# Two opening loads moved to ScalarE's queue, with another hand-written list of steps

## The chip, the cores and the metric

The kernel runs on one core of one Trainium2 chip. The metric is the time of one execution on the device, in microseconds. An execution is one launch that computes both blocks of the reference below from inputs in device memory to an output in device memory.

The core has five engines with queues of their own, each working through its instructions in order: TensorE (PE in the profile) for matmuls, VectorE (DVE), ScalarE (ACT), GpSimd (POOL) and SyncE (SP), which here only issues DMAs. ScalarE can issue DMAs too. Semaphores order the engines among each other.

## The reference

A transformer block on 2048 tokens of width 640: a layer norm, an attention with a compressive memory over four segments of 512 tokens, an output projection with a residual, a second layer norm and a feed-forward block of width 1728 with a residual. All tensors are bfloat16.

```python
def _A_ref(x, wq, wk, wv, wo, beta):          # x is the normalised input
    H, Dh, N, L = 32, 20, 4, 512
    q, k, v = ...                              # (x @ w), split in heads and segments
    phi = lambda t: jnp.where(t > 0, t + 1.0, jnp.exp(t))
    ...
    for s in range(N):
        p = softmax(qs @ ks.T * Dh**-0.5 + causal_mask)
        a_dot = p @ vs
        a_mem = (phi(qs) @ M) / (phi(qs) @ z + 1e-6)
        o = g * a_mem + (1.0 - g) * a_dot      # g = sigmoid(beta), per head
        M = M + phi(ks).T @ vs
        z = z + sum(phi(ks))
    return o @ wo

h  = x + _A_ref(layernorm(x), wq, wk, wv, wo, beta)
h2 = h + silu(layernorm(h) @ w1) @ w2
```

## The kernel before

Tokens lie in 16 blocks of 128, four blocks to a segment. A program written in Python declares some 1,400 steps, each with its engine or engines, what it reads and writes, and the buffers that it takes. It then goes through the table `ORDER`, a long string that names every step once, in order, with the engine where there is a choice (`/A` ScalarE, `/D` VectorE, `/G` GpSimd, `/S` SyncE) and the numbers of the buffers that it takes. `schedule` (from line 302) only reads that table; no planner runs. Steps are emitted in the table's order, so each engine's queue is the part of the table that belongs to it, and a class called `Tracker` adds the waits that reads and writes need.

The names in the table that matter here: `x0`, `x1`, `x2`, `x4`, `x8`, `x12` load blocks of tokens from that block on (one, one, two, four, four, four blocks). `w_q0`, `w_q1`, `w_q2` load the query weights in three parts of 128, 256 and 256 rows, `w_k0` and `w_k1` the key weights in two; `w_w1_0` to `w_w1_4` and `w_w2_0` to `w_w2_5` load the feed-forward weights. `n1_stB`, `n1_rB`, `n1_apB` are the statistics, the reciprocal root and the normalising of block B for the first layer norm, `n2_` the same for the second. For blocks 0 to 3 the transposing is done by TensorE (`n1_tp`, copied out by `n1_te`), for all others by a DMA (`n1_tr`, `n2_tr`). `ot` transposes the attention's output and `kt` phi of the keys, also by DMA. `re_wq` and `re_wk` copy the loaded weights into the order of heads that the projections `pr` need. `vt` and `vp` are DMAs that copy the remaining rows of queries and keys, and of phi of the queries, to the partitions where TensorE wants them. `qk` are the scores, `e` their exponentials (a `+` makes one instruction of 2048 columns in place of two of 1024), `mk` the causal masks, `av` the product with the values, `wo`, `h1`, `h2` the later matmuls. `fill` are matmuls on zeros.

In the opening, SyncE issues every load. Block 0's statistics are taken by VectorE (line 742), those of block 1 by ScalarE (lines 734 and 737), whose first instruction is a table load. VectorE then prepares the root for block 1 (line 753), GpSimd takes it (line 763), VectorE normalises (line 769), TensorE transposes (line 778), and after the copy and the first rearranged query weights (line 694) the projections begin (lines 871 and 866). While this goes on, TensorE runs 30 fillers.

The loads' engine is the last argument of `load_x` (line 575) and `load_w` (line 580), which hand it to `dma`. Each engine's DMAs have one hardware queue: SyncE's is q1, ScalarE's q10. The w2 buffer holds the queries and keys of the first segment until they are used (`QZ`, `QZV`), so the loads of w2 wait for the scores of that segment, and what stands behind them on SyncE waits too.

Of the kernel before, what the change touches and what calls it, by code (L numbers as in the profile page):

```python
# [11 lines left out]
PE, AC, DV, PO, SP = "pe", "act", "dve", "pool", "sp"  # L12
# [312 lines left out]
D = 640  # L325
# [43 lines left out]
mk4x1_384 ve02/D lsc2 lsc3 oe0x/D:0 mk4x2_0 mk4x2_256 av2x:7 ex041:1 oe2x/D:1 kt02:0 n1_tr6 mk0y1_256 mm2 kt00:1 v11:0
qk4x30:2 e4x30:3 pha011:0 ve11/D:1 tn0x:6 nm0x:3 e4x32 mk4x3_0 pha031:1 qk0ya0:0 mk4x3_256 n1_ap7:2 mk4x3_384 v12:6  # L370
e0ya+:4 w_w1_2 ve12/D av4x:4 oe4x/D:0 mz00:5 ma00/A:2,5 qk1ya0:0 e1ya2:0 tn2x:6 nm2x:0 av6x:7 oe6x/D:1 e1ya0 tn4x:6
nm4x:1 qk2ya0:2 kvz e2ya2:1 tn6x:7 mm3 nm6x:2 n1_tr4 v10:0 n1_st11:2 e2ya0 qk0y20:4 e0y2+:6 w_w1_3 w_w1_1 mk0y2_0
kg00/G:0 mk0y2_256 n1_tr7 v13:2 n1_r11/G qk3ya0:4 e3ya0:3 ve10/D n1_st9:6 n1_r9/D pha041:2 ex031:2 mm6 ve13/D ot1:0
wo1:0 n1_st8:3 e3ya2 ot0 ex011:0 wo0:2 rs1 n2_st1:0 mk0y1_384 w_w1_4 phb011 qk4ya0:4 e4ya0:2 n2_r1/D kg02/G e4ya2 rs0
n2_ap1:0 n2_st0:0 pr101:0 qe101/A:0 av0y:1 qk0y30:2 e0y3+:0 w_w2_0/S pr120:6 zf0 n2_r0/D oe0y/D:0 pr100:7 mk0y3_0
ex101:0 qk5ya0:2 n2_ap0:3 e5ya2:4 n2_tr1:0 phb041 qe100/D e5ya0 qe120/D:0 pr121:0 qe121/D qk4y10:4 mk0y3_256 tn0y:1
nm0y:3 e4y10:5 e4y12 mk0y3_384 n1_r8/D av2y:0 oe2y/D:1 qk6ya0:2 mk4y1_0 pha120:0 pr141:1 qe141/D:0 phb031 n2_tr0
h1_0_7_0:6 e6ya+:0 th0_7_0:0 s0_7_0:0 h1_0_12_0:0 th0_12_0:1 qk7ya0:1 e7ya+:1 kt01:0 w_w2_5 h1_0_4_0:7 tn2y:5 s0_12_0
h1_0_3_0:6 kg01/G mk4y1_256 n1_st10:1 th0_3_0:0 mk4y1_384 qvz h1_0_6_0:0 qk4y20:1 th0_4_0:1 nm2y:3 s0_4_0 mm4
h1_0_5_0:5 e4y2+:3 s0_3_0 pr110:7 qe110/D:0 th0_5_0:1 qk4y30:1 pr140:6 th0_6_0:0 e4y32:6 mk4y2_0 e4y30 w_w2_1/S  # L380
mk4y2_256 s0_6_0 s0_5_0 mk4y3_0 mk4y3_256 qe140/D av4y:0 kt03:1 kg03/D ex120:1 qk8a0:4 e8a0:2 e8a2 pr111:1 h1_0_1_0:2
th0_1_0:1 oe4y/D:0 h1_0_8_0:3 th0_8_0:0 qe111/D vt10/S:0 qk8e0:4 s0_1_0 n1_ap8:3 e8e0:4 s0_8_0 mz01:0 ma01/D:3,1
mk4y3_384 av6y:1 e8e2 zf1 qk8b0:2 e8b+:5 kh03/D oe6y/D:1 h1_0_10_0:0 th0_10_0:0 tn4y:6 mzc6 n1_ap9:0 mk8e_0 nm4y:2
tn6y:7 kt04:1 mk8a_0 phb120 nm6y:0 ex100:2 pr130:1 qe130/D:0 qk9a0:3 e9a+:0 s0_10_0 kg04/D pr131:2 qe131/D mk8b_0
pha131:0 h1_0_2_0:7 w_w2_2/S kh04/D th0_2_0:1 mm5 h1_0_11_0:1 th0_11_0:0 s0_11_0 qk9b0:2 e9b0:1 s0_2_0 h1_0_0_0:0
mz02:6 pha101:1 vt13/S mk8b_384 th0_0_0:0 e9b2 mk9a_0 mk9b_0 mk8e_256 h1_0_9_0:7 th0_9_0:1 s0_0_0 ma02/D:0,4,6,7
qk10a0:0 e10a0:3 mzc2 h1_0_13_0:6 h2_0_0:4 e10a2 w_w2_4 ot3 h2_0_1 mk9b_384 mk10a_0 phb101 n1_r10/D pha111:2 vt19/S
mzc0 mb00:0,0 w_w2_3/S s0_9_0 n1_ap11:2 pha100:0 phb100 th0_13_0:0 s0_13_0 ex131:0 phb131 pha110:0 n1_ap10:1 vt12/S
qk10b0:0 e10b+:6 epsg1 av8:7 oe8/D:0 n1_tr8:0 av9:6 oe9/D:1 n1_tr9 ex110:0 phb110 vt18/S vt110/S h2_0_2 mk10b_0
mk10b_384 qk10e0:0 e10e2:2 e10e0 n1_tr11 h2_0_3 ex121:0 h2_1_0:6 o0 kt13:0 qk11a0:2 pha121:0 phb121 wo3:0 rs3 n2_st3:3  # L390
mk10e_0 mk10e_256 h2_1_1 e11a+:4 mk11a_0 vt14/S qk11b0:2 kg13/G:0 ex130:1 tn8:0 e11b+:5 h2_1_2 vt11/S h2_1_3 pha140:0
nm8:1,1 o1 kh13/G n2_r3/G ex111:2 phb111 mm1 n2_ap3:2 mk11b_0 mk11b_384 pha130:0 vt16/S mzc1 vt111/S ot2 qk12a0:2
# [70 lines left out]
def build(nc, es, A_x, A_wq, A_wk, A_wv, A_wo, A_beta, B_x, B_w1, B_w2, out):  # L463
# [10 lines left out]
    G = Graph(pools)  # L474
# [48 lines left out]
    mt = sb("mt", [128, V4], F32)  # L523
    zpad = sb("zpad", [128, 256], BF16)
# [48 lines left out]
    sT0 = G.alloc("sT")  # L573
# [851 lines left out]
```

## Time and profile before

| | |
|---|---|
| three runs, us | 297.7, 298.06, 300.65 (median 298.06) |
| profiled execution's own time, us | 298.33 |
| its span, first to last instruction, us | 296.6 |
| granted TensorE clock, mean | 1.000 |
| DMA queue q1 (SyncE) | 48204 packets, 23.18 MB |
| DMA queue q10 (ScalarE) | 1668 packets, 1.74 MB |
| read from and written to device memory | 10.41 MB and 2.62 MB |

The profile is one execution, taken by the hardware profiler. Times in its rows count from the span's start. A row of the timeline merges instructions of one kind that follow each other; a row that ends in "q" and a line number, such as SPq L578, is the issue of DMAs by that engine, not their transfer. Matmuls are pipelined and their ends are modelled, so TensorE's busy time is a little generous. What ended a wait is inferred from semaphore events; for a wait on several, the last is named.

### The profile page before, as it was taken

Reading aid. Unit: us, or ns where it says so; the run is one execution under the profiler, and the core shown is the slowest. Engines: PE = TensorE matmul, PEld = TensorE weight load, DVE = VectorE, ACT = ScalarE, POOL = GpSimd, SP = SyncE. Lnnn points to the kernel's source line nnn. Section 1 sums busy time; section 2 is a strip of 40 time slices with the busy share of each in tenths; the row PEclk is TensorE's granted clock in tenths of the full one; section 3 lists DMA queues with packets and bytes.
Section 4 is the critical chain, followed back from the end, with each engine's and each line's share of the span. In section 5 each row is a group of like instructions: output and inputs, shape, how many; then the busy total and the mean of one; then the engine's idle time right before and its main releaser. Section 6 shows DMA issues by size and latency. Waiting matters only on the chain.

```text
span 296.6 us, 7437 instructions
## 1 busy us (share of the span) xinstructions
PE 285.0 (96%) x2991; PEld 167.6 (56%) x2991; DVE 222.8 (75%) x506; ACT 217.5 (73%) x266; POOL 139.9 (47%) x257
## 2 busy tenths in 40 slices
PE   7897879999999999999999999999999999999997
PEld 5775445545665455566643444465665457764575
DVE  3897889768989789899678967759967688626522
ACT  5875979999999899999879999788759751014400
POOL 6246834744656477646525656355576620200000
PEclk9999999999999999999999999999999999999999
DMA  7968772804943321254462400154181023220002
GB/s 208 366 209 114 192 105 68 221 18 98 168 89 75 74 39 26 37 111 66 97 140 51 77 1 2 26 75 88 20 102 32 0 59 76 68 67 25 22 22 91
DMA packets 49906, 25.40 MB, mean 86 GB/s; under 512 B 39488, under 2 KB 48032, under 8 KB 49872
## 3 DMA queue, kind: packets, MB, share of 16 engines
q1 hardware_dynamic: 48204, 23.18, 37.3%
q10 hardware_dynamic: 1668, 1.74, 1.9%
q8 instruction: 24, 0.39, 0.6%
q14 instruction: 10, 0.08, 0.1%
HBM read 10.41 MB, written 2.62 MB: 44 GB/s over the span
## 4 chain that ended last, share of the span: by engine, by line
PE 76%; DVE 8%; DMA 7%; ACT 4%; POOL 2%; issue 2%; SPq 1%; DVEq 0%; ACTq 0%
PE ps_all L1349 19%; PE ps_all L1307 15%; PE ps_all L866 12%; PE ps_all L1272 7%; PE ps_all L964 7%; PE ps_all L827 5%; PE ps_all L1008 5%; ACT PT L976 3%; DMA x_tok<-in_A_x_dram 3%; DMA xT<-xn_rot 2%; PE ps_all L1038 1%; DMA w_sb<-w_sb 1%; PE ps_all L1092 1%; PE ps_all L1225 1%; POOL PT L987 1%
## 5 line engine op out<-in xcount | busy, mean ns | idle before, releaser
L976 ACT ACTIVATE PT<-ps_all 128x1024 bf16<-128x1024 f32 (+1 forms) x120 | 153.1, 1310 | 17.7 <-PE ps_all L964 16.5
L987 POOL TENSOR_SCALAR_AFFINE_SELECT PT<-PT 128x512 bf16<-128x512 bf16 x128 | 81.5, 647 | 59.1 <-ACT PT L976 57.0
L1349 PE MATMUL ps_all<-w_sb,sT 128*128 128x320 bf16 (+2 forms) x462 | 64.9, 295 | 0.0
L1307 PE MATMUL ps_all<-hT,w_sb 128*128 128x512 bf16 (+1 forms) x325 | 63.0, 337 | 0.5 <-DVE sT L1322 0.4
L1316 ACT ACTIVATE th<-ps_all 128x512 f32<-128x512 f32 (+2 forms) x70 | 34.0, 505 | 35.1 <-PE ps_all L1307 31.0
L1349 PEld LDWEIGHTS ps_all<-w_sb,sT 128*128 128x128 bf16 x462 | 43.2, 98 | 18.3 <-issue 1.8
L1322 DVE SCALAR_TENSOR_TENSOR sT<-th,ps_all 128x512 bf16<-128x512 f32 (+2 forms) x70 | 37.8, 561 | 17.1 <-ACT th L1316 16.1
L1307 PEld LDWEIGHTS ps_all<-hT,w_sb 128*128 128x128 bf16 x325 | 29.8, 98 | 25.9 <-issue 3.2
L763 POOL TENSOR_TENSOR rst<-rst,eps_c 128x1 f32<-128x1 f32 x32 | 18.4, 579 | 25.1 <-DVE rst L757 23.5
L742 DVE BATCH_NORM_STATS2 stt<-x_tok 128x6 f32<-128x320 bf16 x62 | 27.2, 481 | 1.8 <-DMA x_tok<-in_A_x_dram 1.4
L1362 DVE SCALAR_TENSOR_TENSOR x_tok<-ps_all,x_tok 128x640 bf16<-128x640 f32 (+3 forms) x18 | 13.3, 745 | 16.7 <-PE ps_all L1349 16.6
L1070 POOL TENSOR_TENSOR otok<-on 128x320 bf16<-128x320 bf16 x24 | 19.0, 796 | 11.5 <-DVE on L1062 11.5
L1272 PE MATMUL ps_all<-wo_sb,oT 128*128 128x320 bf16 x160 | 23.8, 299 | 0.0
L883 DVE CAST QK<-ps_all 128x512 bf16<-128x512 f32 x23 | 15.7, 688 | 8.8 <-PE ps_all L866 8.7
L1062 DVE TENSOR_TENSOR on<-ps_all,rd 128x640 bf16<-128x640 f32 x24 | 19.8, 825 | 0.9
L827 PE MATMUL ps_all<-wv_sb,xT 128*128 128x320 bf16 x120 | 18.3, 299 | 1.6 <-DMA xT<-xn_rot 1.3
L1272 PEld LDWEIGHTS ps_all<-wo_sb,oT 128*128 128x128 bf16 x160 | 15.0, 98 | 7.2 <-issue 1.8
L866 PE MATMUL ps_all<-xT,wkr 128*128 128x512 bf16 x75 | 18.7, 380 | 0.0
L866 PE MATMUL ps_all<-xT,wqr 128*128 128x512 bf16 x75 | 18.2, 380 | 0.0
L842 DVE CAST Vx<-ps_all 128x640 bf16<-128x640 f32 x15 | 12.3, 819 | 5.9 <-PE ps_all L827 5.8
L1008 PE MATMUL ps_all<-PT,Vx 128*32 128x512 bf16 (+3 forms) x384 | 16.4, 301 | 0.1
L769 DVE TENSOR_SCALAR xn_rot<-x_tok,mvt,rst 128x640 bf16<-128x640 bf16 x32 | 14.8, 473 | 1.7 <-POOL rst L763 1.0
(106 smaller groups left out, 338.3 us busy)
## 6 DMA issues: line engine op xcount, KB each, us to landing
w_sb<-in_B_w_dram SPq DMA_DIRECT2D x5, 432.0 KB, 6.1
x_tok<-in_A_x_dram SPq DMA_DIRECT2D x3, 640.0 KB, 8.4
w_sb<-in_B_w_dram SPq DMA_DIRECT2D x3, 480.0 KB, 4.4
out_dram<-x_tok ACTq DMA_DIRECT2D x8, 160.0 KB, 1.8
out_dram<-x_tok SPq DMA_DIRECT2D x7, 160.0 KB, 2.0
QKV<-QK SPq DMA_DIRECT2D x12, 72.0 KB
wo_sb<-in_A_wo_dram SPq DMA_DIRECT2D x1, 800.0 KB, 10.0
sT<-in_A_wq_dram SPq DMA_DIRECT2D x2, 320.0 KB, 4.3
```

Source lines behind the costliest of these rows:

```text
L742: T.add(DV, lambda e, hh=hh: e.bn_stats(out=stt[:, s, 6 * hh:6 * hh + 6], in_=xb[:, 320 * hh:320 * hh + 320]), reads=R((xa, xsub)), writes ...
L827: fns.append(lambda e, c=c, hh=hh: e.matmul(bank(ps, hh)[:, 0:320], lhsT=xT_[:, c, 128 * i:128 * i + 128], rhs=wv_sb[:, c, 320 * hh:320 * ...
L866: fns = [lambda e, kc=kc: e.matmul(bank(ps)[:, lo:hi], lhsT=wt[:, kc, c, :], rhs=xT_[:, kc, lo:hi], start=(kc == 0), stop=(kc == NC - 1)) ...
L964: fns.append(lambda e, j=j, o=o, r=r, q0=q0, q1=q1, qa=qa, ka=ka: e.matmul(ps_all[:, o:o + q1 - q0], lhsT=ka[32 * r:32 * r + DH, 128 * j:1 ...
L976: T.add(AC, lambda e: e.activation(out=pt[:, pta.slot, q0:q0 + nq, 0:width], in_=sc3[:, b0:b0 + nq, 0:width], func=ACT.Exp, scale=SCALE), ...
L987: T.add(PO, lambda e: e.affine_select(out=v, in_=v, pattern=[[0, 4], [1, 128]], compare_op=ALU.is_ge, fill=0.0, base=0, channel_multiplier ...
L1008: fns.append(lambda e, j=j, r=r, h=h, pa=pa, pt=pt, co=co, q0=q0, ji=ji: e.matmul(bank(po)[32 * r:32 * r + 32, q0:hi], lhsT=Vx[:, vx.slot, ...
L1272: fns.append(lambda e, c=c, hh=hh: e.matmul(bank(ps, hh)[:, 0:320], lhsT=oT[:, c, 128 * i:128 * i + 128], rhs=wo_sb[:, c, 320 * hh:320 * h ...
L1307: fns = [lambda e, c=c: e.matmul(bank(ps)[:, lo:hi], lhsT=w1_sb[:, c, 128 * f:128 * f + 128], rhs=hT[:, c, lo:hi], start=(c == 0), stop=(c ...
L1316: T.add(AC, lambda e: e.activation(out=th[:, tha.slot, lo:hi], in_=bank(ps)[:, lo:hi], func=ACT.Tanh, scale=0.5), reads=R((ps, [0])), writ ...
L1322: T.add(DV, lambda e: e.scalar_tensor_tensor(out=sT[:, f, lo:hi], in0=th[:, tha.slot, lo:hi], scalar=1.0, in1=bank(ps)[:, lo:hi], op0=ALU. ...
L1349: fns.append(lambda e, f=f, t0=t0, fr=fr, hh=hh, n=n: e.matmul(bank(pa, hh)[:, 0:n], lhsT=sT[:, f, t0:t0 + 128], rhs=w2_sb[:, fr, c0 + 320 ...
```

## The change

Two loads go to ScalarE, and the table is another one.

```diff
-    load_x(0, 1, -100, 2.30, "fix", (SP,))
+    load_x(0, 1, -100, 2.30, "fix", (AC,))
     load_x(1, 1, -100, 2.33, "fix", (SP,))
     for k, w, raw, cuts in (("q", A_wq, 0, (0, 1, 3, 5)), ("k", A_wk, 1, (0, 2, 5))):
         for n, (c0, c1) in enumerate(zip(cuts, cuts[1:])):
             load_w(f"{k}{n}", wraw[:, raw, c0:c1, :], cw(w[128 * c0:128 * c1, :]), -96, 1.4 * (c1 - c0),
-                   [(sT0, [f"{k}{n}"])], "fix", (SP,))
+                   [(sT0, [f"{k}{n}"])], "fix", (AC,) if k == "q" and n == 1 else (SP,))
```

```diff
 ORDER = """
-epsg0:0 vpad0 zpad w2z/G:0 fill30:7 warm iota mt mta mtb mm7 x0:0 x1:4 mm0 n1_st1/A:0,0 w_q0:0 w_q1 w_q2 epsc sel
...
+vpad1:0 zpad fill30:7 iota sel x0:0 w2z/G:0 x1:3 w_q1:0 warm w_q0 vpad0 n1_st0/D:3,0 epsc n1_st1/A:0 halfc n1_r0/G
...
```

All other lines of the table are replaced as well. It names the same steps, apart from exponentials of which eight become one instruction in place of two (`e0y1`, `e8a`, `e10a`, `e16e`, `e18e`, `e24e`, `e25b`, `e30a`) and five become two in place of one (`e13b`, `e20b`, `e21b`, `e23b`, `e28b`), and apart from the fillers at the end, 12 matmuls in place of 2. TensorE has the same number of rows, in nearly the same order.

On ScalarE, the start of the program; `x_tok` is `x0`, `sT` (which holds the raw weights at first) is `w_q1`, and lines 734 and 737 are the statistics of block 1:

```order
 L206 UNCONDITIONAL_BRANCH
+L578 DMA x_tok<-in_A_x_dram 128x640
+L581 DMA sT<-in_A_wq_dram 128x2x640
 L598 ACT_TABLE_LOAD
 L598 ACTIVATE wj<-zpad 128x1
 L734 ACTIVATE otok,mvt<-x_tok 128x640
 L737 ACTIVATE otok,mvt<-x_tok,mvt 128x640
```

Both DMAs now stand ahead of the table load. On SyncE, the same place; the first row was `x0` and `x1` and is now `x1` alone, and the two query parts of 256 rows become one:

```order
-L578 DMA x_tok<-in_A_x_dram 128x640 x2
+L578 DMA x_tok<-in_A_x_dram 128x640
 L581 DMA sT<-in_A_wq_dram 128x640
-L581 DMA sT<-in_A_wq_dram 128x2x640 x2
+L581 DMA sT<-in_A_wq_dram 128x2x640
 L581 DMA sT<-in_A_wk_dram 128x2x640
 L581 DMA sT<-in_A_wk_dram 128x3x640
```

Everything behind them stands two DMAs nearer to the start. The third place is SyncE from its first DMA transpose (`n1_tr5`) to the first load of w2, before the change; line 798 are transposes of normalised blocks, 1207 those of phi of the keys, 1264 those of the attention's output, 581 the loads of weights:

```order
L798 DMA_TRANSPOSE xT<-xn_rot 128x5x128
L1207 DMA_TRANSPOSE phiKt<-phiK 128x4x128
L798 DMA_TRANSPOSE xT<-xn_rot 128x5x128
L1207 DMA_TRANSPOSE phiKt<-phiK 128x4x128
L581 DMA w1_sb<-in_B_w1_dram 128x1728
L798 DMA_TRANSPOSE xT<-xn_rot 128x5x128
L581 DMA w1_sb<-in_B_w1_dram 128x1728 x2
L798 DMA_TRANSPOSE xT<-xn_rot 128x5x128
L1264 DMA_TRANSPOSE oT<-otok 128x5x128 x2
L581 DMA w1_sb<-in_B_w1_dram 128x1728
L581 DMA w2_sb<-in_B_w2_dram 128x4x640
L798 DMA_TRANSPOSE hT<-xn_rot 128x5x128 x2
```

The same stretch after the change:

```order
L798 DMA_TRANSPOSE xT<-xn_rot 128x5x128 x2
L1207 DMA_TRANSPOSE phiKt<-phiK 128x4x128 x2
L581 DMA w1_sb<-in_B_w1_dram 128x1728 x2
L798 DMA_TRANSPOSE xT<-xn_rot 128x5x128
L581 DMA w1_sb<-in_B_w1_dram 128x1728
L798 DMA_TRANSPOSE xT<-xn_rot 128x5x128
L1264 DMA_TRANSPOSE oT<-otok 128x5x128 x2
L581 DMA w1_sb<-in_B_w1_dram 128x1728
L798 DMA_TRANSPOSE hT<-xn_rot 128x5x128
L1207 DMA_TRANSPOSE phiKt<-phiK 128x4x128
L581 DMA w1_sb<-in_B_w1_dram 128x1728
L798 DMA_TRANSPOSE hT<-xn_rot 128x5x128
```

Two w1 loads have moved ahead of the third transpose. The first part of w1 (`w_w1_0`), which before was loaded in the opening right behind beta, is now the last w1 row here, ahead of the second transpose of the second layer norm, `n2_tr0`. The load of w2 has moved behind both of those transposes. Further on, `x12` stands with more scores and exponentials between it and the first statistics that use it, and some casts change between ScalarE and VectorE.

198 lines of the change are left out of this document (99 added, 99 removed).

## The prediction, made before the run

> **What bounds the kernel now.** I read the page's first part, then busy time by stretches, then the chain of waits and the timeline where TensorE is idle. The page's shares come first, then eight stretches (length, then busy microseconds and instructions of each engine, granted clock, DMA share, GB/s).
>
> ```profile
> PE 285.0 (96%) x2991; PEld 167.6 (56%) x2991; DVE 222.8 (75%) x506; ACT 217.5 (73%) x266; POOL 139.9 (47%) x257
> ...
> 0.00:8.30 8.30, 5.80 (x41) 4.18 (x42) 3.32 (x13) 4.55 (x10) 4.96 (x19) 1.00 0.73 224
> 8.30:20.00 11.70, 11.65 (x138) 9.38 (x139) 10.78 (x41) 10.85 (x22) 4.41 (x10) 1.00 0.95 330
> 20.00:45.00 25.00, 20.62 (x274) 12.86 (x273) 20.77 (x50) 18.14 (x19) 15.59 (x30) 1.00 0.76 127
> 45.00:100.00 55.00, 53.67 (x680) 30.84 (x678) 47.85 (x114) 52.61 (x61) 30.29 (x57) 1.00 0.47 103
> 100.00:150.00 50.00, 49.77 (x578) 29.25 (x571) 41.48 (x96) 44.56 (x57) 30.88 (x53) 1.00 0.34 65
> 150.00:200.00 50.00, 49.22 (x469) 23.44 (x468) 37.59 (x79) 44.85 (x49) 26.61 (x44) 1.00 0.30 52
> 200.00:250.00 50.00, 49.75 (x512) 29.14 (x511) 39.11 (x80) 33.97 (x40) 24.48 (x40) 1.00 0.33 56
> 250.00:294.10 44.10, 44.10 (x316) 28.36 (x315) 21.63 (x41) 7.93 (x14) 2.72 (x6) 1.00 0.17 48
> ```
>
> The granted clock is 1.00 throughout, so the clock plays no part. TensorE is idle 1.33 us from 45 to 100, 0.23 to 150, 0.78 to 200, 0.25 to 250 and 0 after that (length less busy time): 2.59 us in 249. The large losses lie early: up to 8.30 us TensorE has only fillers and two transposes, and from 20 to 45 it is idle for 25.00 − 20.62 = 4.38 us. A list that keeps the same work can win little after 45 us, and can lose there without limit.
>
> The opening, from the timeline (start, length, then in brackets the idle time before and what ended it); SPq is an issue of DMAs by SyncE.
>
> ```profile
> 0.80 1.28 ACT L598 ACT_TABLE_LOAD   x1 [0.80 <-PEq L1410]
> ...
> 0.81 0.88 SPq L578 DMA_DIRECT2D x_tok<-in_A_x_dram  x2
> ...
> 1.73 1.42 SPq L581 DMA_DIRECT2D sT<-in_A_wq_dram  x3
> ...
> 2.10 0.20 ACT L598 ACTIVATE wj<-zpad 128x1 f32<-128x1 bf16 x1
> ...
> 3.13 0.89 DVE L742 BATCH_NORM_STATS2 stt<-x_tok 128x6 f32<-128x320 bf16 x2
> ...
> 3.61 0.74 ACT L734 ACTIVATE otok<-x_tok 128x640 bf16<-128x640 bf16 x1 [1.31 <-DMA x_tok<-in_A_x_dram]
> ...
> 5.43 0.15 DVE L753 TENSOR_SCALAR rst<-mvt 128x1 f32<-128x1 f32 x1 [1.17 <-ACT otok L737]
> ...
> 7.74 1.45 DVE L694 COPY wqr<-sT 128x400 bf16<-128x400 bf16 x9
> ...
> 8.30 0.72 PE L871 MATMUL ps_all<-hT,wqr 128*128 128x128 bf16 x10 [0.94 <-DVE wqr L694]
> ```
>
> The chain is: block 1 of x lands, ScalarE starts its statistics at 3.61, VectorE waits 1.17 us for them, and normalising, transposing and the rearranged weights lead to the first projection at 8.30. From there to 20 us TensorE is busy 11.65 of 11.70 us. So what the opening gains shifts everything up to the next wait.
>
> **The change, part by part.** *The two loads.* On SyncE both loads of x took 0.88 us to issue, 0.44 each; block 1 is now SyncE's first DMA and starts 0.44 us earlier. Its statistics also need ScalarE, which now issues two DMAs before its table load.
>
> ```profile
> L1367 ACTq DMA_DIRECT2D out_dram<-x_tok x10: 338/338/455, 215.4 to 294.6; - x10
> ...
> L914 ACTq DMA_DIRECT2D w_sb<-w_sb x4: 701/856/1626, 18.5 to 23.1; - x4
> ...
> x_tok<-in_A_x_dram SPq DMA_DIRECT2D x2, 160.0 KB, 2.3
> sT<-in_A_wq_dram SPq DMA_DIRECT2D x2, 320.0 KB, 4.3
> ```
>
> The nearest row of that size on ScalarE is 0.34 us (minimum, median and maximum, in ns). So ScalarE is ready at 0.80 + 2 × 0.34 + 1.28 + 0.20 = 2.96, or 3.14 with SyncE's 0.43. Block 1 lands at 0.81 + 2.3 = 3.11 by its own row. Statistics start at about 3.2 in place of 3.61: −0.4 us. Bounds: −0.5 (0.81 + 2.3 alone), and on the other side +0.65, if the first DMA that ScalarE issues costs the 1.63 us that its first one in this trace took (0.80 + 1.63 + 0.34 + 1.28 + 0.20 = 4.25). I take −0.4, since 1.63 is one of four and of another shape. The Trainium skill's page "ScalarE: Activation LUTs" gives about 2.7 µs for the table load in its section Terms and about 1283 ns in What ACT_TABLE_LOAD costs. This trace has 1.28 us; by 2.7 the statistics would start near 4.5 and the term would be +0.9 instead.
>
> Block 0 now lands from the other queue. VectorE takes its statistics at 3.13 and later waits 1.17 us for ScalarE's, so a delay of up to a microsecond is covered. The query weights: their third part was issued at about 2.7 and by the 4.3 us of its row landed near 7.0, under VectorE's use at 7.74; now it is issued a microsecond earlier (two issues of 0.44 and 0.47 are gone ahead of it), and the use moves by 0.4. The second part, on ScalarE, lands at about 1.2 + 4.3 = 5.5. No cost. The key weights, x2 and the value weights start 0.9 us earlier; the stretch from 8.30 to 20 moves 330 GB/s at a DMA share of 0.95, so little of this reaches their landing: 0.
>
> *The list between 20 and 45 us.* Three waits, from the timeline; ACT and SPq rows beside them.
>
> ```profile
> 27.77 0.40 PE L964 MATMUL ps_all<-w_sb 20*128 20x256 bf16 x12 [1.55 <-DMA w_sb<-w_sb]
> ...
> 31.09 0.59 SPq L581 DMA_DIRECT2D w_sb<-in_B_w_dram  x1
> 31.72 1.25 SPq L798 DMA_TRANSPOSE xT<-xn_rot  x1
> 33.02 1.05 SPq L581 DMA_DIRECT2D w_sb<-in_B_w_dram  x2
> 35.03 1.21 SPq L798 DMA_TRANSPOSE xT<-xn_rot  x1
> ...
> 34.07 0.40 PE L964 MATMUL ps_all<-w_sb 20*128 20x256 bf16 x8 [0.87 <-DVE otok L1137]
> ...
> 42.45 1.53 PE L827 MATMUL ps_all<-wv_sb,xT 128*128 128x320 bf16 x10 [1.31 <-DMA xT<-xn_rot]
> ```
>
> At 27.77 TensorE waits for the last of the twelve copies of query and key rows. In both lists SyncE issues eight of them and ScalarE four, and the last ones follow the last cast of a projection; all of this moves with the opening. One issue more or less in its order is 0.71 us at most; I take 0. The wait of 0.87 at 34.07: the scores there take PSUM banks that the exponentials before them still hold; the new list gives those exponentials banks 4 to 7 and the next scores 0 to 3, so that it falls away, but TensorE would only reach the next wait sooner. It is worth nothing by itself.
>
> The gate is at 42.45, where a transpose issued at 35.03 lands 7.4 us later, behind three loads of w1 (31.09 and 33.02). The new list has three w1 loads ahead of it too, but issues two before the third transpose and one before the fourth (the second piece of SyncE's order, above), and its own normalised block is ready earlier. If the queue sets the landing, it stays at 42.4 and the 0.4 of the opening is lost: 0 in all. If not, 0.4 + 1.31 = 1.7 are won. I take the middle, −0.8 for opening and gate together.
>
> *w1's first part* is no longer loaded in the opening but directly before the transpose n2_tr0, just ahead of the first h1 matmuls.
>
> ```profile
> w_sb<-in_B_w_dram SPq DMA_DIRECT2D x5, 432.0 KB, 6.1
> ...
> 43.18 7.15 SPq L581 DMA_DIRECT2D w_sb<-in_B_w_dram  x2
> 50.38 2.58 SPq L798 DMA_TRANSPOSE hT<-xn_rot  x2
> 53.00 1.27 SPq L1207 DMA_TRANSPOSE phiKt<-phiK  x1
> ...
> 56.84 1.26 PE L1307 MATMUL ps_all<-hT,w_sb 128*128 128x256 bf16 x10
> ```
>
> Before, SyncE stood from 43.8 to 50.33 behind a w2 load (the 7.15 us); that load now comes after both transposes, so the first can go earlier. I put the issue of w1's first part after it and after a transposed phiK (1.27), near 51.5, and its landing 4 to 6.1 us later, at 55.5 to 57.6; TensorE asks at 56.84 − 0.4 = 56.4. Bounds 0 to +1.2. I take 0, as the DMA queue then holds no other large load.
>
> *x12.* The load of the last four blocks, from the timeline:
>
> ```profile
> 150.51 0.41 SPq L578 DMA_DIRECT2D x_tok<-in_A_x_dram  x1
> ...
> 156.47 0.89 DVE L742 BATCH_NORM_STATS2 stt<-x_tok 128x6 f32<-128x320 bf16 x2 [1.39 <-DMA x_tok<-in_A_x_dram]
> ...
> 158.21 1.25 PE L1307 MATMUL ps_all<-hT,w_sb 128*128 128x512 bf16 x5 [0.38 <-DVE sT L1322]
> ```
>
> VectorE stands 1.39 us before the statistics and TensorE loses 0.38. The new list puts more scores, exponentials and phiQ copies between load and statistics: −0.3, bounds −0.38 and 0.
>
> *The rest.* The new list keeps TensorE's rows and reorders neighbours; eight exponentials of 1024 columns become single ones of 2048 and five the reverse, and several casts change sides. Of the 2.59 − 0.38 = 2.2 us idle after 45 it may remove half (−1.1) or double them (+2.2). I take +0.2, since there is more room above than below. At the end twelve fillers stand where two stood; two take 0.38 us there, twelve at most 2.3, from 294.1 to 296.4, inside the 296.6 that the last store sets: 0.
>
> ```profile
> 294.12 0.38 PE L619 MATMUL ps_all<-zpad 128*128 128x256 bf16 x2
> ```
>
> Sum against the profiled execution's own 298.33 (span 296.6, 1.7 around it): −0.8 − 0.3 + 0.2 = −0.9, so 297.4. The median of the runs, 298.06, is 0.27 below that execution, within the runs' scatter; I leave the sum as it is.
>
> **Rivals.** *No gain (298.3, chance 0.26).* Two loads in flight at once share the DMA engines: block 1 then lands when both are through, at 3.61 as before, and the gate at 42.45 holds what is left. For it: the stretch to 8.30 already has a DMA share of 0.73. Against: block 0 alone was through at 3.13, half a microsecond ahead of block 1, at only 224 GB/s, where the next stretch reaches 330. The Trainium skill's page "DMA: Bandwidth & Descriptors", section Issuing engines are not separate DMA queues, says that DMAs of several engines run on the same 16 DMA engines and that a second issuer saves only the sequencer's time. By that rule this rival is the outcome as far as the bytes decide; no run here shows two loads side by side.
>
> *Slower (300.5, chance 0.22).* w1's first part comes late. Price: if the first transpose is issued no earlier than the 50.38 of before, it, a phiK transpose and the load follow at 50.38 + 1.25 + 1.27 = 52.9; with 6.1 us to landing that is 59.0, 2.6 us after TensorE asks at 56.4, with ScalarE idle behind it. 298.33 − 0.4 + 2.6 = 300.5. It decides from an issue later than 56.4 − 6.1 = 50.3 at that landing time, or 52.4 at 4 us. Against it: SyncE is no longer held by w2.
>
> *Much faster (295.0, chance 0.10).* The waits of 1.55, 0.87, 1.31 and 0.38 fall away with the 0.4: at most 4.5; 298.33 − 3.3 with three quarters of it. Against: the first and third are DMA chains with unchanged contents.
>
> My forecast, 297.4, has 0.42.
>
> **How the numbers follow.** The likeliest case gives 297.4. A measurement of this kernel tells about 1% from no change, 3 us around 298.06: faster is under 295.1, slower over 301.0. Faster: most of the third rival, 0.09. Slower: the second rival with the rest doubled as well (300.5 + 2.2), about half of it, 0.12. Within 1%: 0.79. The range runs from 295.7 (a little above the fast rival) to 300.6 (the slow one), leaving out about 0.1 on each side.
>
> **What would show it.** In the changed profile ScalarE's statistics should start near 3.2 and the first projection near 7.9; the value projection now at 42.45 between 40.7 and 42.4 with a shorter wait; h1 near 56 without a wait for a DMA; no wait of VectorE for x12; TensorE's idle time after 45 us near 2.5. The prediction is wrong if ScalarE's first issue takes over a microsecond, if the fourth transpose lands after 42.4, if the first h1 waits for w1, or if the stretches after 100 us, idle for 1.3 us now, hold several new waits.

## The result and the profile after

| | before | changed |
|---|---|---|
| median, us (22 runs each) | 298.04 | 299.68 |
| lowest and highest, us | 297.35, 300.65 | 298.15, 301.19 |
| profiled execution, its own time and span, us | 298.33, 296.6 | 298.66, 296.9 |
| ratio, with its 95% interval | | 1.0051 [1.0035, 1.0068] |

The changed kernel is 0.5% slower. 299.68 lies inside the range forecast and inside the 1% called no change; the direction and the point, 297.4, were wrong. The profiled execution is among the quickest of the changed kernel: it shows 0.3 us of the 1.6 between the medians. So second profiles of both kernels were taken. In some executions (six of the 35 of before in each of two groups of the experiments below, four of the six with block 0 back on SyncE) the granted clock reads 0.994 and most of the times are 1 to 3 us longer; without them no ratio of the two groups moves by more than 0.0011, and that of block 0 back on SyncE falls by 0.004.

The stretches of the changed kernel, with the columns as before:

```profile
0.00:8.30 8.30, 6.26 (x40) 4.41 (x40) 4.87 (x12) 4.41 (x9) 5.02 (x19) 1.00 0.79 256
8.30:20.00 11.70, 11.47 (x137) 9.23 (x138) 10.54 (x40) 9.28 (x20) 3.53 (x7) 1.00 0.79 269
20.00:45.00 25.00, 21.52 (x280) 13.34 (x277) 20.89 (x52) 21.79 (x23) 17.94 (x31) 1.00 0.66 129
45.00:100.00 55.00, 53.08 (x672) 31.04 (x678) 45.16 (x106) 51.86 (x57) 30.66 (x67) 1.00 0.49 105
100.00:150.00 50.00, 48.22 (x561) 28.82 (x563) 40.85 (x94) 44.43 (x57) 29.79 (x50) 1.00 0.37 68
150.00:200.00 50.00, 48.31 (x463) 23.87 (x470) 38.72 (x79) 45.63 (x52) 26.96 (x46) 1.00 0.33 53
```

From 20 to 45 us TensorE idles 3.48 us, 0.90 less than before; from 45 on it idles more in every stretch, most from 100 to 150 (1.78 for 0.23) and from 150 to 200 (1.69 for 0.78). This trace has 2978 matmul records for 3001 weight loads, before it was 2991 for 2991; 23 matmuls are missing from it and count in part as idle time, so these differences are upper bounds.

The opening, from the timeline:

```profile
0.80 0.42 ACTq L578 DMA_DIRECT2D x_tok<-in_A_x_dram  x1
...
1.25 0.46 ACTq L581 DMA_DIRECT2D sT<-in_A_wq_dram  x1
...
1.74 1.28 ACT L598 ACT_TABLE_LOAD   x1 [1.74 <-PEq L1410]
...
3.70 0.74 ACT L734 ACTIVATE otok<-x_tok 128x640 bf16<-128x640 bf16 x1 [0.47 <-DMA x_tok<-in_A_x_dram]
...
3.88 0.89 DVE L742 BATCH_NORM_STATS2 stt<-x_tok 128x6 f32<-128x320 bf16 x2 [0.42 <-DMA x_tok<-in_A_x_dram]
...
5.52 0.15 DVE L753 TENSOR_SCALAR rst<-mvt 128x1 f32<-128x1 f32 x1 [0.51 <-ACT otok L737]
...
8.44 0.55 PE L871 MATMUL ps_all<-hT,wqr 128*128 128x128 bf16 x7 [0.93 <-DVE wqr L694]
```

ScalarE was ready at 3.24, near the 3.14 forecast, and then waited 0.47 us for block 1, which landed no earlier than before (3.70 for 3.61); the statistics of block 0 start 0.75 later (3.88 for 3.13). The first projection starts at 8.44 for 8.30.

Where TensorE now waits, from its timeline:

```profile
34.43 0.40 PE L964 MATMUL ps_all<-w_sb 20*128 20x256 bf16 x8 [1.37 <-DVE Vx L842]
...
43.44 0.40 PE L964 MATMUL ps_all<-w_sb 20*128 20x256 bf16 x8 [0.37 <-ACT PT L976]
...
107.59 0.70 PE L1307 MATMUL ps_all<-hT,w_sb 128*128 128x256 bf16 x5 [0.26 <-issue]
...
109.16 0.32 PE L1038 MATMUL ps_all<-Mzb,phiQv 128*128 128x84 bf16 x4 [0.54 <-DMA phiQv<-phiQ]
...
150.23 1.02 PE L1307 MATMUL ps_all<-hT,w_sb 128*128 128x512 bf16 x4 [1.05 <-DVE rd L1061]
...
171.89 1.24 PE L866 MATMUL ps_all<-xT,wkr 128*128 128x512 bf16 x5 [0.53 <-issue]
```

The value projection waits for no transpose any more, but the last four waits are in neither profile of before. The one at 109.16 is not wholly new, though: two more traces of the list of before (those of the loads alone and of block 1 first, below) wait 0.40 for the same copies. The wait at 150.23 is some 0.2 us shorter than shown: the record of the first of its five matmuls is missing, which is probably why its row names VectorE. A DMA is named for one of the four only; the other three (two on h1, one on the projection) read what a DMA transpose of SyncE writes. Here is SyncE's timeline, first of the changed kernel, then of before:

```profile
91.93 6.91 SPq L927 DMA_DIRECT2D phiQv<-phiQ  x9
...
101.58 0.78 SPq L927 DMA_DIRECT2D phiQv<-phiQ  x1
102.40 0.51 SPq L1367 DMA_DIRECT2D out_dram<-x_tok  x1
102.96 1.21 SPq L798 DMA_TRANSPOSE hT<-xn_rot  x1
104.22 0.67 SPq L927 DMA_DIRECT2D phiQv<-phiQ  x1
104.93 1.21 SPq L798 DMA_TRANSPOSE hT<-xn_rot  x1
106.18 0.58 SPq L1367 DMA_DIRECT2D out_dram<-x_tok  x1
106.81 0.77 SPq L927 DMA_DIRECT2D phiQv<-phiQ  x1
...
142.71 4.72 SPq L798 DMA_TRANSPOSE hT<-xn_rot  x3
```

```profile
92.27 1.58 SPq L927 DMA_DIRECT2D phiQv<-phiQ  x2
...
95.31 2.25 SPq L927 DMA_DIRECT2D phiQv<-phiQ  x3
...
100.67 0.69 SPq L927 DMA_DIRECT2D phiQv<-phiQ  x1
101.41 1.22 SPq L798 DMA_TRANSPOSE hT<-xn_rot  x1
102.67 0.67 SPq L927 DMA_DIRECT2D phiQv<-phiQ  x1
103.39 1.20 SPq L798 DMA_TRANSPOSE hT<-xn_rot  x1
104.63 3.52 SPq L927 DMA_DIRECT2D phiQv<-phiQ  x5
...
144.56 1.20 SPq L798 DMA_TRANSPOSE hT<-xn_rot  x1
```

TensorE needs all twelve copies of phiQ at one step, its first product with phiQv. In the list of before, seven of the twelve stand ahead of the second transpose and five behind it; `vp13`, a copy of twelve rows, is the first of the row at 92.27. In the new list eleven stand ahead of the second transpose, and `vp13` is the last of all, at 106.81, behind two stores and both transposes; TensorE asks for it at 108.6. In time that is not late: before, the last of the five is issued at about 107.5. But there the product stood behind one more group of h1, from TensorE's timeline,

```profile
108.93 0.72 PE L1307 MATMUL ps_all<-hT,w_sb 128*128 128x256 bf16 x5
109.60 0.31 PE L1038 MATMUL ps_all<-Mzb,phiQv 128*128 128x84 bf16 x4
```

which the new list has behind the product. The second of the two transposes (`n2_tr3` now, `n2_tr2` before) is issued at 104.93 for 103.39, with four more copies ahead of it and a store directly ahead of the pair. Near 143 three transposes of the second layer norm now stand directly one behind the other, and the last is issued at 146.1, where before they were spread and the last began at 144.56. The last of these transposes lands 52.2 to 52.7 us after the start of `qk13a0` (a step near 95 us, see the next table) in the four traces of the list of before, and 54.9 to 56.8 us after it in the seven traces in which the new list is unaltered here.

How long TensorE takes between the same steps of the lists (differences of start times in each trace; `qk13a0` and `qk20a0` are scores, `av30` a product with the values) puts the loss in one place:

| us | start to qk13a0 | to qk20a0 | to av30 | to the end |
|---|---|---|---|---|
| before | 94.96 | 58.69 | 78.47 | 64.5 |
| before, second profile | 94.78 | 58.65 | 78.53 | 64.5 |
| list of before, loads alone | 94.16 | 58.92 | 78.58 | 64.5 |
| list of before, block 1 first | 94.62 | 59.14 | 78.36 | 64.5 |
| changed | 94.18 | 59.91 | 78.37 | 64.5 |
| changed, second profile | 94.95 | 60.03 | 78.40 | 64.5 |
| list alone | 95.34 | 61.00 | 77.86 | 64.5 |
| block 0 back on SyncE | 95.99 | 60.23 | 78.01 | 64.5 |
| edit near 109 | 95.53 | 59.15 | 78.01 | 64.5 |
| only vp13 of it | 94.58 | 60.09 | 78.03 | 64.5 |
| only the transposes of it | 94.15 | 59.73 | 78.53 | 64.5 |
| edit near 149 | 95.30 | 59.38 | 78.21 | 64.5 |
| both, and a third edit | 94.89 | 59.41 | 79.54 | 64.5 |
| both edits | 94.29 | 58.63 | 78.17 | 64.5 |
| both edits, again | 94.81 | 59.44 | 78.17 | 64.5 |
| both edits, loads on SyncE | 95.71 | 59.48 | 78.06 | 64.5 |

From 95 to 154 us the changed kernel needs 1.2 to 1.4 us more than the two profiles of before, and 0.8 to 1.4 us more than all four traces of that list; elsewhere it gains and loses within 0.8, no more than two profiles of one kernel differ. The rows other than those of before and of the changed kernel are experiments told below.

### The profile page after: what moved, and what is told of

It is laid out like the page before. It is cut to its first block, busy times and chain, and to the rows that moved or that the text cites. A ratio compares the mean times of both kernels' runs of the same rounds, so it can differ in the third digit from the quotient of the medians.

```text
span 296.9 us, 7441 instructions
## 1 busy us (share of the span) xinstructions
PE 283.9 (96%) x2978; PEld 169.3 (57%) x3001; DVE 220.1 (74%) x494; ACT 219.8 (74%) x267; POOL 141.6 (48%) x265
## 4 chain that ended last, share of the span: by engine, by line
PE 78%; ACT 11%; DVE 4%; issue 2%; DMA 2%; SPq 1%; ACTq 1%; POOL 0%
PE ps_all L1349 21%; PE ps_all L1307 17%; PE ps_all L866 9%; ACT PT L976 9%; PE ps_all L1272 7%; PE ps_all L964 7%; PE ps_all L827 6%; PE ps_all L1008 5%; PE ps_all L1038 1%; DMA x_tok<-in_A_x_dram 1%; PE ps_all L1225 1%; PE ps_all L1042 1%; PE ps_all L1301 1%; DMA phiQv<-phiQ 1%; ACT th L1316 1%
## 5 line engine op out<-in xcount | busy, mean ns | idle before, releaser
L1307 PE MATMUL ps_all<-hT,w_sb 128*128 128x512 bf16 (+1 forms) x316 | 61.0, 336 | 2.4 <-DVE rd L1061 1.1
L1070 POOL TENSOR_TENSOR otok<-on 128x320 bf16<-128x320 bf16 x24 | 19.6, 818 | 13.1 <-DVE on L1062 13.1
L866 PE MATMUL ps_all<-xT,wkr 128*128 128x512 bf16 x68 | 17.2, 379 | 1.4 <-issue 1.0
L760 POOL TENSOR_TENSOR rst<-mvt,eps_c 128x1 f32<-128x1 f32 x23 | 4.7, 204 | 27.8 <-DVE mvt L745 24.8
L866 PE MATMUL ps_all<-xT,wqr 128*128 128x512 bf16 x68 | 16.9, 380 | 0.4 <-issue 0.2
L1280 DVE TENSOR_TENSOR x_tok<-ps_all,x_tok 128x640 bf16<-128x640 f32 x16 | 13.0, 810 | 5.5 <-PE ps_all L1272 5.4
```

Of the source, the lines that this page charges most:

```text
L866: fns = [lambda e, kc=kc: e.matmul(bank(ps)[:, lo:hi], lhsT=wt[:, kc, c, :], rhs=xT_[:, kc, lo:hi], start=(kc == 0), stop=(kc == NC - 1)) ...
L1307: fns = [lambda e, c=c: e.matmul(bank(ps)[:, lo:hi], lhsT=w1_sb[:, c, 128 * f:128 * f + 128], rhs=hT[:, c, lo:hi], start=(c == 0), stop=(c ...
```

## The experiments

Every time stands against runs of the kernel before on the same chip.

| kernel | median, us (runs) | ratio to before, 95% interval |
|---|---|---|
| new list, both loads on SyncE | 300.56 (6) | 1.0078 [1.0050, 1.0106] |
| list of before, both loads on ScalarE | 298.16 (12) | 1.0002 [0.9985, 1.0020] |
| changed, block 0 back on SyncE | 301.26 (6) | 1.0125 [1.0086, 1.0165] |
| changed, again | 299.71 (11) | 1.0054 [1.0036, 1.0072] |
| edit near 109 | 298.36 (12) | 0.9995 [0.9972, 1.0018] |
| edit near 149 | 299.12 (12) | 1.0027 [1.0006, 1.0047] |
| both, and a third edit | 299.89 (12) | 1.0046 [1.0024, 1.0068] |
| before, block 1 loaded first | 297.95 (12) | 0.9991 [0.9972, 1.0011] |
| both edits | 297.97 (12) | 0.9989 [0.9962, 1.0016] |
| both edits, again | 298.87 (12) | 1.0023 [1.0000, 1.0047] |
| both edits, loads on SyncE | 299.27 (12) | 1.0030 [1.0005, 1.0055] |
| only vp13 of the edit near 109 | 299.35 (12) | 1.0025 [1.0000, 1.0050] |
| only the transposes of it | 298.75 (12) | 1.0017 [0.9990, 1.0045] |
| before, again | 298.41 (8) | 1.0016 [0.9982, 1.0050] |

**The list alone and the loads alone.** The first keeps the new list and has the engines of before:

```diff
-    load_x(0, 1, -100, 2.30, "fix", (AC,))
+    load_x(0, 1, -100, 2.30, "fix", (SP,))
-... "fix", (AC,) if k == "q" and n == 1 else (SP,))
+... "fix", (SP,))
-... w_q1:0 warm w_q0 ...
+... w_q0:0 w_q1 warm ...
```

> The new list, with both loads back on SyncE. Theory 1 (the list costs, the loads do nothing): the time stays near the changed kernel's 299.7, 1.2 to 1.8 us above before, and the first projection starts at 8.3 again (statistics of block 1 at 3.6). Theory 2 (the loads cost, the list does nothing): the time falls back to 298.0, within 0.4. Theory 3 (both together only, since the shifted opening makes the list's steps meet badly): about 298.0 to 298.8 here and in the run with the loads alone.

The second keeps the list of before and moves the two loads:

```diff
-... fill30:7 warm iota mt mta mtb mm7 x0:0 x1:4 mm0 n1_st1/A:0,0 w_q0:0 w_q1 w_q2 ...
+... fill30:7 x0:0 w_q1:0 warm iota mt mta mtb mm7 x1:4 mm0 n1_st1/A:0,0 w_q0 w_q2 ...
```

> The list of before with the two loads on ScalarE, directly ahead of its table load. Theory 1: within 0.4 us of before (298.0), with the first projection at about 8.4 and block 0 landing 0.7 later than before. Theory 2: 299.4 to 299.9. Theory 3: 298.0 to 298.8.

The loads alone do nothing (1.0002); the list alone costs 2.5 us, more than the 1.2 to 1.8 expected. The first theory holds in its direction and the second falls. The third falls too, as far as it said that the list alone is harmless. That the list costs more with the loads on SyncE (300.56 against 299.7) was expected by no theory, and with six runs its interval overlaps the changed kernel's; one wait near 150 was longer in its trace, from TensorE's timeline (here, too, the first of five matmuls has no record, so the wait is some 0.2 us shorter):

```profile
152.48 1.02 PE L1307 MATMUL ps_all<-hT,w_sb 128*128 128x512 bf16 x4 [1.83 <-DVE on L1062]
```

**Block 0 back on SyncE.** Only the second part of the query weights stays on ScalarE.

```diff
-    load_x(0, 1, -100, 2.30, "fix", (AC,))
+    load_x(0, 1, -100, 2.30, "fix", (SP,))
```

> The changed kernel with block 0 of x back on SyncE; only the second part of the query weights stays on ScalarE. If two loads of x in flight share the DMA engines (Theory 1's reading of the opening), block 0 lands near 3.1 to 3.3 again, block 1 at 3.6 to 3.7 and the first projection starts at 8.2 to 8.4, so that the time stays within 0.4 us of the changed kernel's. If instead ScalarE's queue itself lands a load late, block 0 is early here (3.1) and block 1 earlier than 3.5, and the first projection gains 0.2 or more.

Neither came. In its timeline of the opening:

```profile
0.80 0.47 ACTq L581 DMA_DIRECT2D sT<-in_A_wq_dram  x1
...
3.78 0.89 DVE L742 BATCH_NORM_STATS2 stt<-x_tok 128x6 f32<-128x320 bf16 x2 [0.32 <-DMA x_tok<-in_A_x_dram]
...
5.11 0.74 ACT L734 ACTIVATE otok<-x_tok 128x640 bf16<-128x640 bf16 x1 [2.30 <-DMA x_tok<-in_A_x_dram]
```

The 320 KB of query weights, issued at 0.80 on the other queue, push block 1 of x from 3.61 to 5.11 and block 0 from 3.13 to 3.78, although SyncE issued both as before. Loads on two queues share what carries them, and a large one issued early on the second queue delays the small ones on the first. The first projection starts at 9.79 for 8.44. In the changed kernel this part goes out 0.45 later, at 1.25, behind block 0, and block 1 is ready at 3.70. The Trainium skill's page "DMA: Bandwidth & Descriptors", section Issuing engines are not separate DMA queues, says that a second issuer brings no second set of DMA engines; this trace agrees, with the 1.50 us that block 1 loses.

**Second profiles, of the changed kernel and of the kernel before.**

> The changed kernel unaltered, for a second profile and more times. Its first profiled execution was 0.3 us longer in span than that of before, while the medians differ by 1.6. If the list leaves waits that come and go with the landing of transfers, the second profile differs from the first by 0.5 us or more, at waits for DMA-fed operands, and its time lies nearer to 299.7. If the first profile was typical, spans agree within 0.3 and the gap between profile and median has another cause.

> The kernel before, unaltered, for a second profile. If the wait of 1.31 at 42.45 was one late landing of that one execution, the value projection there waits under 0.5 now, and the third part of the query weights has landed by 7.2 again. If the wait is usual, it is 1.0 to 1.4 here too.

The second profile of the changed kernel has a span of 297.9, 0.9 more than the first, and the difference arises where operands come by DMA: VectorE waits 0.64 for the key weights at 9.94, where it waited 0.25, and TensorE is 0.35 later by 23 us; its waits near 108 and 110 are 0.55 and 0.53, and one of 0.42 for transposed phi of the keys has come in at 93.46. The second profile of before answers the question on the gate, in TensorE's timeline:

```profile
28.38 0.40 PE L964 MATMUL ps_all<-w_sb 20*128 20x256 bf16 x12 [1.69 <-DMA w_sb<-w_sb]
...
43.72 0.40 PE L964 MATMUL ps_all<-w_sb 20*128 20x256 bf16 x8 [0.48 <-ACT PT L976]
```

The value projection ahead of the second row does not wait; 0.48 for an exponential is what is left of the 1.31. The same 0.48 stands in the profile with the loads alone. One more trace of the list of before, with block 1 loaded first (below), has a part of the wait:

```profile
42.00 1.53 PE L827 MATMUL ps_all<-wv_sb,xT 128*128 128x320 bf16 x10 [0.43 <-DMA xT<-xn_rot]
```

The transpose behind it landed 7.4 us after its issue in the first profile, and 5.7, 5.5 and 6.5 us after it in the other three. So the wait of 1.31, which the prediction took for a gate, was the latest of four landings. The third part of the query weights, the other question, landed by 6.8.

**The order of SyncE near 109.** `vp13` goes forward, and both transposes go ahead of the stores:

```diff
-vp18/S mk13a_0 vp12/S ex141:1
+vp18/S vp13/S mk13a_0 vp12/S ex141:1
...
-tn11:5 nm11:3,1 kt10:1 pha211:2 vp16/S
+tn11:5 nm11:3,1 kt10:1 n2_tr3 pha211:2 vp16/S
...
-out1/S n2_tr2 mk14a_0 mk12a_0 vp17/S n2_tr3 mz11:5 out0/S v23:6 vp13/S ma11
+n2_tr2 mk14a_0 mk12a_0 vp17/S mz11:5 out1/S out0/S v23:6 ma11
```

> The changed kernel with one stretch of SyncE's order altered: the first of the twelve-row copies of phiQ (vp13) goes from behind two stores to directly behind vp18, and the transposes n2_tr3 and n2_tr2 go ahead of both stores. The theory that the list's SyncE order costs the time says: the waits of TensorE of 0.3 to 0.6 near 108 (h1) and 0.5 near 110 (phiQ) shrink below 0.2 each, TensorE is 0.7 to 1.1 us earlier at 112, and the time falls by 0.5 to 1.1 against the changed kernel's 299.7, to 298.6 to 299.2. The rival, that each wait won is only handed to the next one, says: earlier at 112 but no earlier at 152, and a time within 0.3 of 299.7.

Both waits are gone (0.11 is left on h1), and the median is 0.15 from before; against the changed kernel's ratio of 1.0054 the 0.9995 is 0.6% or 1.7 us, more than expected, with the intervals apart. Not all that was won is handed on: from `qk13a0` to `qk20a0` it takes 59.15 where the changed kernel takes 59.9 to 60.0, about half of the 1.7. Its wait near 150 was 0.21 here without any edit there, and the trace of the edit near 149 (below) has only 0.06 on h1 at 108.5 without any edit there, so part of the gain may be one of landing times. The two halves by themselves:

> The changed kernel with only the copy vp13 moved ahead; both transposes stay between the stores. If the phiQ copy is the wait that counts: the wait of 0.5 near 110 is gone, the one near 108 stays, and the time is 0.4 to 0.9 lower than 299.7. If the transposes count, the wait of 0.3 to 0.6 near 108 grows or the two change places, and the time is within 0.3 of 299.7.

> The changed kernel with only n2_tr3 and n2_tr2 moved ahead of the stores; vp13 stays last. If the transposes count: the wait near 108 is gone, and with vp13 now issued earlier too (nothing but the stores' 1.1 us stands between), the wait near 110 is at most 0.5; the time is 0.4 to 0.9 lower. If vp13 counts, the wait near 110 takes up what is won at 108: within 0.3 of 299.7.

The timeline of TensorE, with `vp13` alone moved and then with the transposes alone moved:

```profile
108.64 0.71 PE L1307 MATMUL ps_all<-hT,w_sb 128*128 128x256 bf16 x5 [0.91 <-issue]
...
150.59 1.24 PE L1307 MATMUL ps_all<-hT,w_sb 128*128 128x512 bf16 x5 [0.98 <-DMA hT<-xn_rot]
```

```profile
108.83 0.32 PE L1038 MATMUL ps_all<-Mzb,phiQv 128*128 128x84 bf16 x4 [0.65 <-DMA phiQv<-phiQ]
...
149.80 1.24 PE L1307 MATMUL ps_all<-hT,w_sb 128*128 128x512 bf16 x5 [1.05 <-DMA hT<-xn_rot]
```

Each half removes its own wait, and the other grows: 0.91 on h1 when the copy is early, 0.65 on the copy when the transposes are. They stand one behind the other in TensorE's order, so that the first hides part of the second, and only both together clear the place. By the stretch from `qk13a0` to `qk20a0` the halves win nothing (60.09) and 0.2 to 0.3 us (59.73). By times (1.0025 and 1.0017) they lie between the changed kernel and both, but their intervals overlap with either. The second rows also name what the wait near 150 is for: the transposes.

**The order near 149.** Blocks 7 and 4 are normalised and transposed earlier, and block 5 is transposed directly after its normalising:

```diff
-n2_tr6:0 qk18a0:1
+n2_tr6:0 n2_r7/G n2_ap7:3 n2_tr7 qk18a0:1
...
-n2_st5:0 n2_r5/G tn17:0 nm17:3,0 kh14/D
+n2_st5:0 n2_r5/G n2_ap4:1 n2_tr4 tn17:0 nm17:3,0 kh14/D
...
-mk19b_0 n2_ap5:2 h2_2_1
+mk19b_0 n2_ap5:2 n2_tr5 h2_2_1
...
-n2_ap4:1 n2_tr5 n2_r7/G n2_ap7:3 phb230 n2_tr4 n2_tr7 vt22/A
+phb230 vt22/A
```

> The changed kernel with the normalising and the transposes of blocks 7, 4 and 5 of the second layer norm moved up one after the other, so that the last is not issued as the third of three in a row. The SyncE theory says: the wait of 0.9 to 1.8 near 150 falls below 0.3 and TensorE is 0.6 to 1.2 earlier at 152; part of it (up to 0.5) may come back at the first statistics of x12 near 157. Time 298.8 to 299.3. The rival of waits handed on: a wait of the same size appears at 157 or 172, and the time stays within 0.3 of 299.7. If the wait near 150 stays as it is, it isn't the transposes that it waits for.

As expected: no wait over 0.23 is left near 150, and the time is 1.0027 of before, 0.3% under the changed kernel's 1.0054, though the intervals overlap a little. The stretch to `qk20a0` is 0.5 to 0.7 us shorter than in the changed kernel (59.38). The wait near 110 is still 0.52, and one of 0.31 for VectorE comes in at 143.6.

**Both, with a third edit, and both alone.** The third edit puts the root and the normalising of block 15 ahead of block 14's:

```diff
-n1_ap13:0 n1_st15:6 mk20e_0
+n1_ap13:0 n1_st15:6 n1_r15/G mk20e_0
...
-th1_2_0:0 s1_5_0 n1_st14:5
+th1_2_0:0 n1_ap15:2 s1_5_0 n1_st14:5
...
-ve30/A:1 n1_r15/G s1_8_0
+ve30/A:1 s1_8_0
...
-kt20:1 mz20:7 n1_ap15:2 kg20/G
+kt20:1 mz20:7 kg20/G
```

> Both of these edits together and a third: root and normalising of block 15 ahead of those of block 14, so that its transpose can be issued earlier (wait of 0.5 near 172). If the waits add up: 1.5 to 2.5 below the changed kernel, 297.2 to 298.2, the time of before or a little under it. If they are handed on: 299.0 to 299.7.

A miss: 299.89, no better than the changed kernel. The timeline shows what the third edit did:

```profile
163.43 0.67 DVE L769 TENSOR_SCALAR xn_rot<-x_tok,mvt,rst 128x640 bf16<-128x640 bf16 x1 [1.00 <-POOL rst L763]
...
164.75 1.25 PE L1307 MATMUL ps_all<-hT,w_sb 128*128 128x512 bf16 x5 [1.09 <-DVE sT L1322]
```

VectorE now stands 1.00 us at the normalising of block 15 and waits for GpSimd's root; a step of the feed-forward block (line 1322) is queued behind it, and TensorE waits 1.09 for that. A wait moved forward takes everything behind it along: from `qk20a0` to `av30` this kernel takes 79.54, and 78.17 without the third edit. The kernels without it:

> The changed kernel with the edits of the stretches near 109 and 149, without the third one. If the third edit (which put VectorE behind a root of GpSimd and TensorE behind that, 1.1 at 164.75) is what spoilt the run of all three, the two together give 297.6 to 298.2, the time of before or 0.5 under it, with no wait over 0.35 between 100 and 160. If the two edits win the same thing, since the wait near 150 was also gone with the edit near 109 alone, it is 298.2 to 298.6, as with that edit alone.

> The kernel with both SyncE edits once more, for a narrower interval against before. If it beats before by anything, the ratio stays at 0.999 or below with an interval under 1.001; if the repaired list is worth just what the old one was, the ratio lies within 0.998 to 1.002.

> The kernel with both SyncE edits, and both loads back on SyncE. With the unrepaired list the loads on ScalarE were worth 0.8 us (299.7 against 300.6), on the list of before nothing. If that came from the wait near 150, which was longer in that execution, it is gone with the repaired order: 297.7 to 298.3 here, within 0.3 of the same list with the loads on ScalarE. If it came from the opening (first projection at 8.67 there), it remains: 298.5 to 298.9, and the first projection starts at 8.6 or later.

The two edits give 297.97 in one measurement, as expected, and 298.87 in another: the time of before, to within 0.3%, and no better. The second measurement is a miss by a little (1.0023, outside both of the expected bands), and its interval overlaps the changed kernel's; the first one's does not. With the loads on SyncE the time of 299.27 is a miss as well, above both bands, and not different from the 298.87 beside it. In that second measurement 12 runs of this list scatter by 1.1 us (standard deviation) and 23 of before by 0.5; in the first, both scatter by 0.9, so it is not shown that this list scatters more. It still has places that hang on a landing: with the loads on SyncE, TensorE's timeline shows this one,

```profile
94.22 0.47 PE L1225 MATMUL ps_all<-Vx,phiKt 128*128 128x84 bf16 x8 [1.20 <-DMA phiKt<-phiK]
```

which was 0.29 in the run of both edits beside it. With the loads on SyncE, the first projection started at 8.29 here and at 8.67 in the unrepaired list, so the 8.67 does not come from where the loads are issued. The 0.8 between the unrepaired list with them and without stays open between the scatter of six runs and the landings.

**Block 1 first.** The kernel before, with the first two loads exchanged:

```diff
-x0:0 x1:4
+x1:4 x0:0
```

> The kernel before with the two first loads in the other order on SyncE: block 1 first, whose statistics on ScalarE are the longer chain. By the opening as read so far, block 1 lands near 3.1 and block 0 near 3.6, the statistics of block 1 start at 3.1 in place of 3.6, and the first projection 0.2 to 0.45 earlier than 8.30. If an earlier opening is worth its length at the end, the time falls by 0.2 to 0.45 (to about 297.7); if waits for transposes and for rows of queries and keys hold it up, TensorE is early at 10 us and not at 45, and the time is within 0.15 of before.

The statistics did start at 3.14: at the head of SyncE's queue, with nothing on ScalarE's, block 1 landed as its row says. But the first projection came later, at 8.78, for a reason outside the edit. From the timeline, and then the fillers by their tile, here and in the kernel before:

```profile
1.12 6.16 PE L619 MATMUL ps_all<-zpad 128*128 128x256 bf16 x30 [1.12 <-DVE zpad L596]
...
3.14 0.74 ACT L734 ACTIVATE otok<-x_tok 128x640 bf16<-128x640 bf16 x1 [0.84 <-DMA x_tok<-in_A_x_dram]
...
7.12 0.72 PE L778 MATMUL ps_all<-ident,xn_rot 128*128 128x128 bf16 x10
```

```profile
L619 PE MATMUL ps_all<-zpad x30: 272/421/421, 1.1 to 7.0; 128*128 128x256 bf16 x30
```

```profile
L619 PE MATMUL ps_all<-zpad x30: 272/283/421, 1.1 to 5.7; 128*128 128x256 bf16 x30
```

The first block was normalised by about 6.2, but the 30 fillers ahead of its transposes ran until 7.1, where before they ended at 6.0. So this run says nothing on what an earlier opening is worth; by its median the exchange is worth nothing that can be measured.

## Why the prediction was wrong

**Opening and gate, −0.8: measured 0.** Two steps failed. "Block 1 lands at 0.81 + 2.3" did not hold: the 2.3 us were measured for loads that followed each other on one queue, and with one queue alone they hold (3.14 with block 1 first). With block 0 and then the query weights in flight on the other queue, block 1 was ready at 3.61 to 3.86 in ten traces, as the rival *No gain* had it; no run separates the share of block 0 from that of the weights. And the wait of 1.31 at 42.45 was taken from one execution as if each had it. Of the three other traces of the list of before two have nothing of it and one has 0.43, so there was little to win. ScalarE's issues and table load were summed right: 3.14 with SyncE's issue time, measured 3.24.

**The third part of the query weights, no cost: not always.** It was issued a microsecond earlier, as forecast, and landed at 6.8 in the first profile of the changed kernel. But it landed at 8.0 and 8.4 in two other traces with that opening (the edits near 109 and 149), where VectorE waited 0.08 and 0.52 for it, and the first projection started at 8.72 and 9.04; with the list alone, issued as before, it landed at 8.0 too. In the ten traces it started at 8.40 to 9.04, in the two profiles of before at 8.24 and 8.30.

**The waits at 27.77 and 34.07.** The first was costed at 0. It became 0.31, with a new one of 0.83 at 22.89 ahead of it: moved, and nothing won. The second did not fall away, as foreseen, but grew to 1.37; that it is worth nothing by itself was right, since up to `qk13a0` the lists are level.

**w1's first part, 0: right.** Its issue at 51.2 was near the 51.5 forecast, and the first h1 at 56.36 did not wait for it. The rival *Slower* ended on the right side by another road than its own.

**x12, −0.3: half right.** VectorE's wait is gone, and from `qk20a0` to `qk23a0` TensorE takes 15.41 for 16.17. But 0.5 of it is lost again at 171.89, where the transpose of block 15 lands no earlier than before (171.8 for 171.5); by `av30` 0.1 is left.

**The rest of the list after 45 us, +0.2: this is the step that failed most.** It measured +1.2 to +1.4 against the two profiles of before (+0.8 to +1.4 against all four traces of that list), all of it between 95 and 154 us. The bounds (−1.1 to +2.2) held it, but the value was chosen by feeling, "more room above than below". The prediction compared SyncE's order only up to the second layer norm of the first segment; the same comparison further on shows `vp13` moved from first to last and the transposes moved behind four more copies and directly behind a store. Its last sign of being wrong, several new waits after 100 us, is what came. Edits of just these places, in SyncE's order and in the normalising that feeds it, remove these waits and bring the stretch to 58.6 to 59.5 us, where the unedited list takes 59.9 to 61.0 and that of before 58.7 to 59.1. What the merged exponentials and the exchanged casts cost by themselves was not tested.

**The end, 0: right** (64.5 us from `av30` on in every trace).

## What to carry to other kernels

When a hand-written order is replaced, compare the queue of the engine that issues DMAs over the whole program, and look up for each transfer that moved back when its reader asks for it, since the reader may have moved too: the waits here were 0.3 to 1.1 us each, and TensorE's share of busy time was 96% in both kernels. Before a wait is counted as a gain, see it in a second profile of the same kernel. An earlier issue on another queue is worth only what the transfers in flight leave free; here that was nothing.

## What the hardware showed that was not expected

The 30 fillers at the start took 4.89 us in one trace of before, 5.08 in the other and up to 6.29 in other runs. A filler takes 421 ns at first and 272 later, and the point of change differs between executions, though the granted clock in the rows reads 1.00. Where it comes late, the fillers themselves hold the opening up. The Trainium skill's page "TensorE: Matmul & The Clock Gate", section Part 1: The HAM clock gate, says that the clock is raised after a stretch of activity by a window that runs freely, so that the number of slow matmuls differs from run to run; these durations agree.

The first DMA transpose between 136 and 139 us, with none just ahead of it, landed 2.6 us after its issue in all 16 traces; of the three in a row near 143 the slowest took 4.9 to 5.5 us in five traces of that list and 4.3 and 4.4 in two, and the last, for which TensorE waits, 3.4 to 4.4. With the same instructions there, TensorE waited 0.21 for them in one execution and about 1.6 (1.83 with the missing record) in another.
